# Attention and a GEGLU feed-forward block on one core: splitting each batch into an attention phase and a feed-forward phase, with tiled matmuls and hand-ordered queues

## The chip, the cores and the metric

The kernel runs on one core of a Trainium2 chip. The metric is the device time of one execution in microseconds; a profile's span (first to last instruction) is up to 3 us shorter than the timed run.

The engines are called PE (TensorE, the matrix multiplier), DVE (VectorE), ACT (ScalarE), Pool (GpSimd) and SP (SyncE). "The changed kernel" is the kernel after the change.

## The reference

```python
# attention: B, H, S, Nb, D = 8, 8, 576, 16, 64; 16 "beacon" keys that every query sees, then causal
k_all = concatenate([beacon_k, k], axis=2);  v_all = concatenate([beacon_v, v], axis=2)
scores = where(causal, -1e9, q @ k_all.T / 8)
a = softmax(scores);  x = a @ v_all                       # -> (4608 tokens, 512)
# feed-forward: d_model 512, d_ff 1536
out = (gelu(x @ w_gate) * (x @ w_val)) @ w_out            # float32
```

## The kernel before

Per batch and pair of heads it transposes q and k on PE, computes the scores with the keys on the partitions, adds the causal mask with a matmul of the identity and a mask tile, takes exp on ACT, and multiplies exp (the stationary operand) with v and a column of ones. The result has queries on partitions, so DVE normalises it and PE transposes it back. Feed-forward work for finished tokens is woven in: one "unit" (a gate and value step, or a quarter of an output chunk) after each key tile.

```python
# scores: contraction over all 128 partitions; the other head's 64 rows of q are zero
for hi in range(2):
    nc.tensor.matmul(scs[hi][0:kr, 0:width], kT_sb[0:P, jj*P : jj*P+kr],
                     qT_sb[hi][0:P, s_lo : s_lo+width], start=True, stop=not diag)
if diag:                                   # the mask, as a matmul
    for hi in range(2):
        nc.tensor.matmul(scs[hi][0:kr, 0:Nd], ident[0:kr, 0:kr], mb[0:kr, 0:Nd], start=False, stop=True)
...
# values: exp is stationary, v and a column of ones move (65 columns)
nc.tensor.matmul(x_ps[0:N, hi, :], expT[0:kr, hi, off : off+N], v_sb[0:kr, jj, 2*m+hi, :], ...)
...
nc.vector.reciprocal(...);  nc.vector.tensor_scalar(...)            # for each head
nc.tensor.transpose(xT_ps, xn_sb[0:N, :], ident[0:N, 0:N])          # back to features on partitions
nc.vector.tensor_copy(xT_sb[:, m, n0 : n0+N], xT_ps)
...
# one unit of feed-forward: g_ps and v_ps have one PSUM buffer each while attention runs
nc.scalar.activation(th_sb, g_ps, ACT.Tanh, scale=GELU_TANH_SCALE)
nc.vector.scalar_tensor_tensor(out=p_sb, in0=th_sb, scalar=1.0, in1=g_ps, op0=ALU.add, op1=ALU.mult)
nc.vector.scalar_tensor_tensor(out=hT_sb[:, fi, :], in0=p_sb, scalar=0.5, in1=v_ps, op0=ALU.mult, op1=ALU.mult)
...
for jj in range(N_KT):                     # the weaving
    attn_qk_tile(jj, qT_sb, kT_sb, expT)
    try_emit_ffn(tokens_written, 1)
    if pending:
        attn_av_chunk(*pending.pop(0))
```

The softmax here doesn't subtract the row's maximum and nothing guards it: scores larger than these inputs give would overflow.

Of the kernel before, what the change touches and what calls it, by code (L numbers as in the profile page):

```python
# [8 lines left out]
P = 128  # L9
# [5 lines left out]
N_KT = 5  # L15
N_QT = 5
F_TILES = D_FF // P
K_CHUNKS = D_MODEL // P
N_TOK_CHUNK = 512
N_CHUNKS = N_TOK // N_TOK_CHUNK  # L20
NPAIR = H // 2

S_LO = [0, 112, 240, 368, 496]
S_N = [112, 128, 128, 128, 80]
KROWS = [128, 128, 128, 128, 80]

GELU_TANH_SCALE = 0.7978845608028654

PASSES = [(0, 0, 512), (0, 512, 64), (1, 112, 464), (2, 240, 336), (3, 368, 208), (4, 496, 80)]
EXP_OFF = [0, 576, 1040, 1376, 1584]  # L30
EXP_W = 1664
QK_SCALE = 0.125
# [4 lines left out]
ALU = mybir.AluOpType  # L37


@with_exitstack  # L40
def kernel(
# [12 lines left out]
    nc = tc.nc  # L54

    const = ctx.enter_context(tc.tile_pool(name="const", bufs=1))
    wpool = ctx.enter_context(tc.tile_pool(name="wpool", bufs=1))
    xpool = ctx.enter_context(tc.tile_pool(name="xpool", bufs=1))
    inpool = ctx.enter_context(tc.tile_pool(name="inpool", bufs=3))
    tpool = ctx.enter_context(tc.tile_pool(name="tpool", bufs=2))  # L60
    epool = ctx.enter_context(tc.tile_pool(name="epool", bufs=3))
    npool = ctx.enter_context(tc.tile_pool(name="npool", bufs=4))
    fpool = ctx.enter_context(tc.tile_pool(name="fpool", bufs=2))
    hpool = ctx.enter_context(tc.tile_pool(name="hpool", bufs=2))
    opool = ctx.enter_context(tc.tile_pool(name="opool", bufs=2))

    ident = const.tile([P, P], BF16, name="ident", tag="ident")
    make_identity(nc, ident)
    NEG = -30000.0
    mb_std = const.tile([P, P], BF16, name="mb_std", tag="mb_std")  # L70
    mb0 = const.tile([P, 112], BF16, name="mb0", tag="mb0")
    nc.gpsimd.memset(mb_std, 0.0)
    nc.gpsimd.affine_select(
        out=mb_std,
        in_=mb_std,
        pattern=[[1, P]],
        compare_op=ALU.is_ge,
        fill=NEG,
        base=0,
        channel_multiplier=-1,  # L80
    )
    nc.gpsimd.memset(mb0, 0.0)
    nc.gpsimd.affine_select(
        out=mb0,
        in_=mb0,
        pattern=[[1, 112]],
        compare_op=ALU.is_ge,
        fill=NEG,
        base=16,
        channel_multiplier=-1,  # L90
    )

    wg_sb = wpool.tile([P, K_CHUNKS, D_FF], BF16, name="wg_sb", tag="wg_sb")
    wv_sb = wpool.tile([P, K_CHUNKS, D_FF], BF16, name="wv_sb", tag="wv_sb")
    wo_sb = wpool.tile([P, F_TILES, D_MODEL], BF16, name="wo_sb", tag="wo_sb")

    def load_weights():
        nc.gpsimd.dma_start(
            out=wg_sb, in_=moe_w_gate.rearrange("(kk p) f -> p kk f", p=P)
        )  # L100
        nc.gpsimd.dma_start(
            out=wv_sb, in_=moe_w_val.rearrange("(kk p) f -> p kk f", p=P)
        )
        nc.gpsimd.dma_start(
            out=wo_sb, in_=moe_w_out.rearrange("(ii p) m -> p ii m", p=P)
        )

    xT_sb = xpool.tile([P, NPAIR, N_TOK], BF16, name="xT_sb", tag="xT_sb")

    dma_jobs = []  # L110

    def load_batch(b):
        q_sb = inpool.tile([P, N_KT, H, D], BF16, name="q_sb", tag="q_sb")
        k_sb = inpool.tile([P, N_KT, H, D], BF16, name="k_sb", tag="k_sb")
        v_sb = inpool.tile([P, N_KT, H, D + 1], BF16, name="v_sb", tag="v_sb")

        def dma(out_ap, in_ap):
            nc.gpsimd.dma_start(out=out_ap, in_=in_ap)  # L118

        hsets = [(0, 2), (2, H)] if b == 0 else [(0, H)]  # L120
        nc.gpsimd.memset(v_sb[:, :, :, 64:65], 1.0)
        for (h0, h1) in hsets:
            hs = slice(h0, h1)
            for j in range(4):
                dma(q_sb[:, j, hs, :], q[b, hs, j * P : (j + 1) * P, :].rearrange("h p d -> p h d"))
            dma(q_sb[0:64, 4, hs, :], q[b, hs, 512:576, :].rearrange("h p d -> p h d"))
            dma(k_sb[0:NB, 0, hs, :], beacon_k[b, hs, :, :].rearrange("h t d -> t h d"))
            dma(k_sb[NB:P, 0, hs, :], k[b, hs, 0:112, :].rearrange("h p d -> p h d"))
            for j in range(1, 4):
                r0 = 112 + (j - 1) * P  # L130
                dma(k_sb[:, j, hs, :], k[b, hs, r0 : r0 + P, :].rearrange("h p d -> p h d"))
            dma(k_sb[0:80, 4, hs, :], k[b, hs, 496:576, :].rearrange("h p d -> p h d"))
            dma(v_sb[0:NB, 0, hs, 0:64], beacon_v[b, hs, :, :].rearrange("h t d -> t h d"))
            dma(v_sb[NB:P, 0, hs, 0:64], v[b, hs, 0:112, :].rearrange("h p d -> p h d"))
            for j in range(1, 4):
                r0 = 112 + (j - 1) * P
                dma(v_sb[:, j, hs, 0:64], v[b, hs, r0 : r0 + P, :].rearrange("h p d -> p h d"))
            dma(v_sb[0:80, 4, hs, 0:64], v[b, hs, 496:576, :].rearrange("h p d -> p h d"))
        return q_sb, k_sb, v_sb

    ph1 = ExitStack()
    ph1.__enter__()
    psum_sc = ph1.enter_context(tc.tile_pool(name="psum_sc", bufs=2, space=bass.MemoryType.PSUM))
    psum_x = ph1.enter_context(tc.tile_pool(name="psum_x", bufs=2, space=bass.MemoryType.PSUM))
    psum_gv = ph1.enter_context(tc.tile_pool(name="psum_gv", bufs=1, space=bass.MemoryType.PSUM))
    pools = {"g": (psum_gv, "g"), "v": (psum_gv, "v"), "o": (psum_x, "x")}

    qpers = ctx.enter_context(tc.tile_pool(name="qpers", bufs=1))
    qTA0_tiles = []
    qT0B_tiles = []  # L150
    for r in range(2):
        ta = qpers.tile([P, S], BF16, name=f"qTA0_{r}", tag=f"qTA0_{r}")
        tb = qpers.tile([P, S], BF16, name=f"qT0B_{r}", tag=f"qT0B_{r}")
        nc.vector.memset(ta[64:128, :], 0.0)
        nc.vector.memset(tb[0:64, :], 0.0)
        qTA0_tiles.append(ta)
        qT0B_tiles.append(tb)
    pair_counter = [0]

    def transpose_pair(q_sb, k_sb, m):  # L160
        r = pair_counter[0] % 2
        pair_counter[0] += 1
        qT_ps = psum_sc.tile([P, 1024], BF16, name="qT_ps", tag="sc0")
        for j in range(4):
            nc.tensor.transpose(
                qT_ps[:, j * P : (j + 1) * P],
                q_sb[:, j, 2 * m : 2 * m + 2, :],
                ident[:, :],
            )
        nc.tensor.transpose(  # L170
            qT_ps[:, 512:576], q_sb[0:64, 4, 2 * m : 2 * m + 2, :], ident[0:64, 0:64]
        )
        qTA0 = qTA0_tiles[r]
        qT0B = qT0B_tiles[r]
        nc.scalar.copy(qTA0[0:64, :], qT_ps[0:64, 0:S])
        nc.scalar.copy(qT0B[64:128, :], qT_ps[64:128, 0:S])  # L176
        kT_ps = psum_sc.tile([P, 1024], BF16, name="kT_ps", tag="sc1")
        for j in range(4):
            nc.tensor.transpose(
                kT_ps[:, j * P : (j + 1) * P],  # L180
                k_sb[:, j, 2 * m : 2 * m + 2, :],
                ident[:, :],
            )
        nc.tensor.transpose(
            kT_ps[:, 512:592], k_sb[0:80, 4, 2 * m : 2 * m + 2, :], ident[0:80, 0:80]
        )
        kT_sb = tpool.tile([P, SK], BF16, name="kT_sb", tag="kT_sb")
        nc.scalar.copy(kT_sb, kT_ps[:, 0:SK])  # L188
        return (qTA0, qT0B), kT_sb

    def attn_qk_pair_start():
        return epool.tile([P, 2, EXP_W], BF16, name="expT", tag="expT")

    def attn_qk_tile(jj, qT_sb, kT_sb, expT):
        kr = KROWS[jj]
        for (pj, s_lo, width) in PASSES:
            if pj != jj:
                continue
            diag = s_lo == S_LO[jj]
            Nd = S_N[jj]  # L200
            scs = [
                psum_sc.tile([P, 512], FP32, name=f"sc{hi}", tag=f"sc{hi}")
                for hi in range(2)
            ]
            for hi in range(2):
                nc.tensor.matmul(  # L206
                    scs[hi][0:kr, 0:width],
                    kT_sb[0:P, jj * P : jj * P + kr],
                    qT_sb[hi][0:P, s_lo : s_lo + width],
                    start=True,  # L210
                    stop=not diag,
                )
            if diag:
                mb = mb0 if jj == 0 else mb_std
                for hi in range(2):
                    nc.tensor.matmul(  # L216
                        scs[hi][0:kr, 0:Nd], ident[0:kr, 0:kr], mb[0:kr, 0:Nd],
                        start=False, stop=True,
                    )
# [52 lines left out]
    def ensure_transposed(b, m):  # L272
        if b >= B:
            return
# [164 lines left out]
```

## Time and profile before

484.34 us (median of 4 runs, 483.44 to 486.26); span 481.2 us.

The page of the profile. The first line gives busy time, share of the span and instruction count of each engine (PEld: weight loads; with PE they add up to 672.5 us in a span of 481.2, so the two overlap); the rows of digits are tenths of busy time, or of the granted PE clock, in 40 equal slices; in the groups, the numbers after the first bar are busy us and mean ns of one, those after the second bar the engine's idle time just before them.

```profile
PE 433.9 (90%) x3384; PEld 238.6 (50%) x3440; DVE 267.6 (56%) x1020; ACT 265.9 (55%) x625; POOL 125.0 (26%) x174
...
PE   2488699999998999989999999999998999999994
...
PEclk9999899999999999999999999999999999999998
...
L334 PE MATMUL o_ps<-wo_sb,hT_sb 128*128 128x512 bf16 x426 | 98.0, 379 | 0.9 <-DVE xT_sb L262 0.6
...
L240 PE MATMUL x_full<-v_sb,expT 128*128 128x65 bf16 (+3 forms) x960 | 60.4, 198 | 0.0
```

PE is the engine to look at, but "90% busy" does not say how much is left to gain, and the mean lengths (379 and 198 ns) do not say what a matmul costs. Records overlap: those of 379 ns start 216 ns apart. The price is the time from one start to the next, 216 ns for 512 columns and 29 ns for most value matmuls. The timeline of PE in the steady state (start us, length us, line, operation, tiles and shapes, count):

```profile
200.06 0.36 PE L206 MATMUL sc_3179<-qTA_1_120,kT_sb 128*128 128x464 bf16 x1
200.26 0.36 PE L206 MATMUL sc_3180<-qT0B_121,kT_sb 128*128 128x464 bf16 x1
200.45 0.22 PE L216 MATMUL sc_3179<-mb_std,ident 128*128 128x128 bf16 x1
200.51 0.22 PE L216 MATMUL sc_3180<-mb_std,ident 128*128 128x128 bf16 x1
200.56 0.31 PE L206 MATMUL sc_3199<-qTA_1_120,kT_sb 128*128 128x336 bf16 x1
...
205.27 0.39 PE L165 MATMUL qT_ps<-ident,q_sb 128*128 128x128 bf16 x4
205.59 0.20 PE L170 MATMUL qT_ps<-ident,q_sb 64*128 64x64 bf16 x1
205.72 0.40 PE L179 MATMUL kT_ps<-ident,k_sb 128*128 128x128 bf16 x4
```

The two heads' scores follow one another, 0.19 us for 464 columns. The second part shows something more: the transpose of q's last 64 rows is recorded with the tile 64\*128, its neighbours with 128\*128. From the start of the matmul before it to its own start pass 151 ns where 55 are usual, and to the next one 132 ns where a matmul of 64 columns takes about 28. So in this trace changing the array's tiling costs about 100 ns each way (96 and 104 here). The 80-row transpose of k that follows (80\*128) shows no such stop: it starts 56 ns after the matmul before it, at 205.96 us, and the next one 40 ns later; it is counted as no change.

A sum over the recorded starts divides the span. "Streaming" is each matmul at its ordinary start-to-start time (216 ns for 512 columns, 89 for 208, 55 to 56 for 128 in this trace, which is 2.4 columns per ns plus 2 to 3 ns; 29 ns or so for the shortest); a change of tiling is the excess at such a place, up to 105 ns; the rest of the excess is waiting. 55 of 1296 feed-forward matmuls are missing from this trace; they are added back at 0.216 us and taken off the waits.

| before, us | |
|---|---|
| feed-forward matmuls, 1296 x 0.2155 | 279 |
| scores and masks | 61 |
| value matmuls | 28 |
| transposes, in and out | 24 |
| 64 changes of tiling | 6 |
| PE waits between its first and last matmul | 71 |
| before the first matmul; after the last | 4; 6 |

About 34 us of the waits lie in the first 60 us. The busy times by stretch (columns: stretch, length, then PE, PEld, DVE, ACT and Pool busy with counts, granted clock, DMA share, GB/s):

```profile
0.00:60.00 60.00, 35.57 (x343) 22.58 (x347) 20.46 (x115) 35.02 (x87) 47.60 (x74) 0.97 1.29 120
60.00:120.00 60.00, 57.96 (x468) 32.26 (x475) 38.03 (x144) 35.32 (x82) 35.69 (x46) 1.00 1.71 128
120.00:420.00 300.00, 286.60 (x2331) 159.71 (x2371) 178.95 (x714) 178.49 (x427) 41.72 (x54) 1.00 0.34 40
```

PE has only 343 matmuls in the first 60 us; the first exp starts at 18.4 us and the first gate matmul at 51.8.

### The profile page before, as it was taken

The page shows a single profiled execution, that of the slowest core. Times are in us where ns is not written, and L with a number is a line of the kernel's source. Part 1 is how long each engine was busy: PE and PEld are TensorE (multiplying, and loading weights), DVE is VectorE, ACT ScalarE, POOL GpSimd, SP SyncE. Part 2 cuts the span into 40 slices and gives each one's busy share as a digit, 9 for nine tenths or more (in the row PEclk, how much of TensorE's full clock was granted, in tenths as well). Part 3 has the DMA queues.
Part 4 walks back from the last instruction along what each step waited for, and adds up shares of the span by engine and source line. Part 5 has one row for each costly group of instructions (what it writes and reads, how often), then busy time and mean ns, then how long its engine had stood idle before and what let it go on. Part 6 is the DMA issues. An engine that isn't in the chain of part 4 may idle for free.

```text
span 481.2 us, 8884 instructions
## 1 busy us (share of the span) xinstructions
PE 433.9 (90%) x3384; PEld 238.6 (50%) x3440; DVE 267.6 (56%) x1020; ACT 265.9 (55%) x625; POOL 125.0 (26%) x174
## 2 busy tenths in 40 slices
PE   2488699999998999989999999999998999999994
PEld 0255455555555555555555455555555554544441
DVE  0056387347843786268625783488437762782850
ACT  2388546665556755584657556655566554332321
POOL 9998129933430415040330300000000000000000
PEclk9999899999999999999999999999999999999998
DMA  4999999998592809054392800200020000200202
GB/s 28 85 119 163 206 173 126 131 157 52 36 67 80 59 2 101 0 111 29 24 78 89 52 1 0 89 1 1 1 89 1 1 0 1 90 0 1 87 1 87
DMA packets 122491, 29.16 MB, mean 61 GB/s; under 512 B 115280, under 2 KB 116816, under 8 KB 122448
## 3 DMA queue, kind: packets, MB, share of 16 engines
q0 software_dynamic: 117696, 19.15, 54.3%
q1 hardware_dynamic: 4752, 9.44, 5.2%
q8 instruction: 27, 0.44, 0.4%
q14 instruction: 16, 0.13, 0.1%
HBM read 38.27 MB, written 9.44 MB: 99 GB/s over the span
## 4 chain that ended last, share of the span: by engine, by line
PE 66%; ACT 13%; POOL 8%; DVE 6%; DMA 4%; issue 2%; ACTq 0%; POOLq 0%
PE o_ps L334 19%; PE g_ps L297 17%; PE v_ps L306 15%; ACT expT L222 4%; DVE p_sb L316 4%; DMA wv_sb<-in_moe_w_val_dram 4%; PE x_full L240 4%; ACT th_sb L314 4%; POOL v_sb L118 3%; POOL k_sb L118 3%; POOL q_sb L118 2%; PE xTf L261 1%; ACT qT0B_121 L176 1%; ACT kT_sb L188 1%; DVE hT_sb L319 1%
## 5 line engine op out<-in xcount | busy, mean ns | idle before, releaser
L297 PE MATMUL g_ps<-xT_sb,wg_sb 128*128 128x512 bf16 x394 | 109.2, 379 | 7.7 <-DMA wg_sb<-in_moe_w_gate_dram 2.3
L306 PE MATMUL v_ps<-xT_sb,wv_sb 128*128 128x512 bf16 x421 | 111.0, 379 | 1.3 <-DMA wv_sb<-in_moe_w_val_dram 0.9
L314 ACT ACTIVATE th_sb<-g_ps 128x512 bf16<-128x512 f32 x108 | 64.4, 598 | 78.4 <-PE g_ps L297 53.8
L316 DVE SCALAR_TENSOR_TENSOR p_sb<-th_sb,g_ps 128x512 bf16<-128x512 bf16 x108 | 74.1, 687 | 51.7 <-ACT th_sb L314 51.5
L334 PE MATMUL o_ps<-wo_sb,hT_sb 128*128 128x512 bf16 x426 | 98.0, 379 | 0.9 <-DVE xT_sb L262 0.6
L249 DVE RECIPROCAL rec_sb<-x_full 128x1 f32<-128x1 f32 (+2 forms) x320 | 36.5, 155 | 99.0 <-PE x_full L240 84.7
L251 DVE TENSOR_SCALAR xn_sb<-x_full,rec_sb 128x64 bf16<-128x64 f32 (+2 forms) x320 | 76.1, 278 | 0.0
L319 DVE SCALAR_TENSOR_TENSOR hT_sb<-p_sb,v_ps 128x512 bf16<-128x512 bf16 x108 | 73.2, 679 | 4.3 <-PE v_ps L306 2.5
L306 PEld LDWEIGHTS <-wv_sb 128*128 128x128 bf16 x432 | 41.6, 98 | 47.9 <-DMA wv_sb<-in_moe_w_val_dram 1.4
L297 PEld LDWEIGHTS <-wg_sb 128*128 128x128 bf16 x432 | 41.2, 97 | 47.6 <-issue 13.7
L334 PEld LDWEIGHTS <-hT_sb 128*128 128x128 bf16 x432 | 40.6, 98 | 46.0 <-issue 1.6
L240 PE MATMUL x_full<-v_sb,expT 128*128 128x65 bf16 (+3 forms) x960 | 60.4, 198 | 0.0
L240 PEld LDWEIGHTS <-expT 128*128 128x128 bf16 (+3 forms) x960 | 51.0, 108 | 17.7 <-issue 0.6
L341 ACT COPY o_sb<-o_ps 128x512 f32<-128x512 f32 x36 | 21.1, 585 | 68.4 <-PE o_ps L334 68.4
L262 DVE COPY xT_sb<-xTf 128x128 bf16<-128x128 bf16 (+2 forms) x160 | 34.4, 215 | 41.9 <-PE xTf L261 41.9
L118 POOL DMA_DIRECT2D q_sb<-in_q_dram x45 | 37.4, 893 | 47.5 <-PE qT_ps L170 47.5
L118 POOL DMA_DIRECT2D k_sb<-in_k_dram x45 | 37.4, 900 | 16.3 <-DMA wo_sb<-in_moe_w_out_dram 8.3
L216 PEld LDWEIGHTS <-ident 128*128 128x128 bf16 (+1 forms) x320 | 29.6, 103 | 17.7 <-issue 7.7
L261 PE MATMUL xTf<-ident,xn_sb 128*128 128x128 bf16 (+2 forms) x160 | 34.8, 217 | 2.6 <-DVE xn_sb L251 2.2
L118 POOL DMA_DIRECT2D v_sb<-in_v_dram x45 | 37.0, 869 | 0.0
L206 PEld LDWEIGHTS <-kT_sb 128*128 128x128 bf16 (+1 forms) x384 | 33.1, 104 | 6.3 <-issue 3.5
L261 PEld LDWEIGHTS <-xn_sb 128*128 128x128 bf16 (+2 forms) x160 | 15.6, 97 | 27.6 <-DVE xn_sb L251 17.0
(1121 smaller groups left out, 488.2 us busy)
## 6 DMA issues: line engine op xcount, KB each, us to landing
out_dram<-o_sb SPq DMA_DIRECT2D x9, 1024.0 KB, 4.4
q_sb<-in_q_dram POOLq DMA_DIRECT2D x28, 128.0 KB, 5.8
k_sb<-in_k_dram POOLq DMA_DIRECT2D x21, 128.0 KB, 4.4
v_sb<-in_v_dram POOLq DMA_DIRECT2D x21, 128.0 KB, 4.8
wg_sb<-in_moe_w_gate_dram POOLq DMA_DIRECT2D x1, 1536.0 KB, 11.5
wv_sb<-in_moe_w_val_dram POOLq DMA_DIRECT2D x1, 1536.0 KB, 18.1
wo_sb<-in_moe_w_out_dram POOLq DMA_DIRECT2D x1, 1536.0 KB, 26.1
k_sb<-in_k_dram POOLq DMA_DIRECT2D x7, 112.0 KB, 4.6
```

The costliest lines, as they stand in the source:

```text
L118: nc.gpsimd.dma_start(out=out_ap, in_=in_ap)
L240: nc.tensor.matmul(x_ps[0:N, hi, :], expT[0:kr, hi, off : off + N], v_sb[0:kr, jj, 2 * m + hi, :], start=(idx == 0), stop=(idx == ntiles - 1),
L249: nc.vector.reciprocal(rec_sb[0:N, hi : hi + 1], x_ps[0:N, hi, 64:65])
L251: nc.vector.tensor_scalar(out=xn_sb[0:N, 64 * hi : 64 * hi + 64], in0=x_ps[0:N, hi, 0:64], scalar1=rec_sb[0:N, hi : hi + 1], scalar2=None, ...
L261: nc.tensor.transpose(xT_ps, xn_sb[0:N, :], ident[0:N, 0:N])
L262: nc.vector.tensor_copy(xT_sb[:, m, n0 : n0 + N], xT_ps)
L297: nc.tensor.matmul(g_ps, wg_sb[:, kk, fi * P : (fi + 1) * P], xT_sb[:, kk, n0 : n0 + N_TOK_CHUNK], start=(kk == 0), stop=(kk == K_CHUNKS - 1),
L306: nc.tensor.matmul(v_ps, wv_sb[:, kk, fi * P : (fi + 1) * P], xT_sb[:, kk, n0 : n0 + N_TOK_CHUNK], start=(kk == 0), stop=(kk == K_CHUNKS - 1),
L314: nc.scalar.activation(th_sb, g_ps, ACT.Tanh, scale=GELU_TANH_SCALE)
L316: nc.vector.scalar_tensor_tensor(out=p_sb, in0=th_sb, scalar=1.0, in1=g_ps, op0=ALU.add, op1=ALU.mult)
L319: nc.vector.scalar_tensor_tensor(out=hT_sb[:, fi, :], in0=p_sb, scalar=0.5, in1=v_ps, op0=ALU.mult, op1=ALU.mult,)
L334: nc.tensor.matmul(o_ps, hT_sb[:, fi, ti * P : (ti + 1) * P], wo_sb[:, fi, :], start=(fi == 0), stop=(fi == F_TILES - 1),)
```

## The change

The intent: fewer streamed columns in attention, fewer and larger instructions on DVE and ACT, no masks and no back-transposes on PE, and an order of every queue written by hand. Each batch becomes an attention phase, filled with the output matmuls of the batch before, and a pure gate-and-value phase.

```diff
-# scores over 128 partitions, q padded with zeros, mask by matmul, exp per head
+# scores: each head on its own 64 rows of the array; one exp for both heads; mask afterwards on Pool
+for hi in range(2):
+    r = slice(64 * hi, 64 * hi + 64)
+    mm(s_ps[:, hi, col : col + w], qkT[r, 1, t * P : (t + 1) * P],
+       qkT[r, 0, NB + s_lo : NB + s_lo + w], True, True)
+act(expT[:, :, o : o + w], s_ps[:, :, 0:w], ACT.Exp, scale=QK_SCALE)
+keep(nc.gpsimd.affine_select(out=d, in_=d, ..., fill=0.0, ...))
...
-# values: exp stationary, [v, 1] moving; reciprocal, scale, transpose back, copy
+# values transposed: v (or ones, for the sums) stationary, exp moving; each head in its own 64 columns
+for hi in range(2):
+    mm(x_ps[64 * hi : 64 * hi + 64, base + q0 : base + q1],
+       v_sb[0:kr, t, 2 * m + hi, :] if base == X0 else ones[0:kr, :],
+       expT[0:kr, hi, e0 : e0 + q1 - q0], first and not (base == Z0 and q0 == 0), last, ...)
+act(ln_sb, x_ps[:, Z0 : Z0 + S], ACT.Ln);  act(rec_sb, ln_sb, ACT.Exp, scale=-1.0)
+keep(nc.vector.tensor_tensor(out=xT_sb[:, m, ...], in0=x_ps[:, X0 : X0 + S], in1=rec_sb, op=ALU.mult))
...
-# feed-forward: Tanh, two vector instructions, one PSUM buffer for g and one for v
+act(ge_sb, gv_ps[:, 0, :], ACT.Gelu)                       # gv_ps: both in one of two buffers
+keep(nc.vector.tensor_tensor(out=h_of[ci][:, fi, :], in0=gv_ps[:, 1, :], in1=ge_sb, op=ALU.mult))
...
+# q and k of batches 0 and 1: four sequence rows in one 1 KB read; DVE undoes the permutation
+if b < NPERM: dma(dst[...], src[b, :, 0:512, :].rearrange("h (p r) d -> p h (r d)", r=4))
...
+for m in range(1, NPAIR):                                  # the order of an attention phase
+    scores(b, m, 0); scores(b, m, 1)
+    av(m - 1, 0, 2); o(4)                                  # o(n): n output matmuls of batch b - 1
+    scores(b, m, 2); av(m - 1, 4, 1, 3)
+    if m < NPAIR - 1: transpose_pair(b, m + 1)
+    o(2); normalize(b, m - 1); scores(b, m, 3); o(2)
```

## The prediction

> **What bounds it now.** The tensor engine (PE). The engine table has PE busy 90%, vector engine 56%, scalar engine 55%. Start-to-start times in the timeline: a 512-column matmul 216 ns, a value matmul 29 ns (38 ns with 80 weight columns). Feed-forward: 1296 × 0.216 = 280 us, unchanged. Attention, per head pair: scores 3328 columns 1.4 us, 10 mask matmuls 0.5, 30 value matmuls 0.95, 10 input transposes 0.5, 5 output transposes 0.3: about 3.7 us, 32 pairs = 120 us. Before and after each 64-row transpose PE loses about 100 ns (151 ns against 55 start to start; 132 against 28); 64 such changes of array tiling cost 6 us. Together 406 of 481 us. The other 75 us are waits: some 40 in the first 60 us (first exp at 18.4 us, first gate matmul at 51.8, 10 feed-forward matmuls by 60 us), the rest spread over the middle, where gate and value products have one PSUM buffer each and tanh and two vector instructions (0.60 + 0.69 + 0.68 us) stand in the loop.
>
> **What changes on PE.** Scores of two heads go to two 64-row tiles and should run together: 1664 columns, 0.72 us. Masks and output transposes go (-0.8 us). Value matmuls stream 1664 columns of exp plus 1664 for sums against ones, two heads in two 64-column tiles: 18 slots, short ones [...] at about 65-70 ns: 1.7 us instead of 0.95. So a pair needs about 2.9 us, 93 us in all. But the program now has 409 changes of tiling instead of 64; at 0.1 us they cost 41 us. [...] PE work: 280 + 93 + 41 = 414 us, slightly more than now.
>
> **What changes elsewhere.** Vector engine: 1020 instructions become about 350, off the path. Gelu (0.6 us) plus one vector multiply (0.69) fit under a 1.73 us gate-and-value step with two buffers, so feed-forward phases run at PE's rate, 20.8 us. In attention phases the scalar engine needs 4.7 us a pair (exps of 1024, 960, 928, 416 elements at 0.17 + 0.00083 per element, then Ln and Exp of 576), PE about 6 with output matmuls between; exchanges of two PSUM buffers leave some waits (about 20 us in the whole), and the single output accumulator a few. Table loads, 1.3 us twice per batch, mostly hide. 1 KB rows and fewer issues bring the first exp to about 12.5 us.
>
> **Sum.** First attention phase ends near 38 us; 8 feed-forward phases at 20.8; 7 attention phases at about 30; last chunk and outputs about 46-49: near 461 us span, 463 us timed. Range 440 to 484. Faster by over 2%: 0.74; within 2%: 0.19; slower: 0.07.
>
> **Signs.** Phases: feed-forward 20-22 us, attention 28-32. First exp 11-14 us. Two heads' score matmuls start under 30 ns apart, and so do long value matmuls; a pair's value matmuls take 1.5-2.0 us. At each change of tiling about 0.1 us beyond streaming. PE gaps at score matmuls waiting for exp.
>
> **What would make it wrong.** Value tiles not overlapping: +35 us (about 500). Scores not overlapping: +14. Short value slots at 110 ns: +15. Changes of tiling at 60 ns: -10; free: -25. The second batch's load landing behind the weights at 45 us instead of 36: +9. Pool's 34 load issues at 0.88 us in the first feed-forward phase delaying the masks of the next batch.

That two tiles run side by side was an assumption, since no trace of the kernel before has two tiles at work together. The 65 to 70 ns for a short value slot were the author's estimate; two value matmuls of the kernel before, at 29 to 38 ns, take 58 to 76.

## The result, and the profile after

465.61 us (median of 4 runs, 465.3 to 466.41); span 463.9 us. Ratios here and below are the mean time of one kernel's fast runs over that of the other's of the same rounds, so not quite the ratio of the medians quoted: 0.961, 95% interval 0.9586 to 0.9635. The change is 3.9% faster.

The page of the changed kernel:

```profile
PE 420.9 (91%) x3248; PEld 201.6 (43%) x3248; DVE 152.7 (33%) x259; ACT 230.9 (50%) x316; POOL 164.1 (35%) x297
...
PE   0577997999999999999999999999999999999985
...
PEclk9987999999999999999999999999999999999999
...
L140 PE MATMUL o_ps<-wo_sb,hT_sb 128*128 128x512 bf16 x432 | 112.8, 381 | 6.9 <-DVE o_sb L302 6.9
...
L140 PE MATMUL x_ps<-expT,ones 128*64 128x144 bf16 (+5 forms) x576 | 49.1, 254 | 0.0
```

DVE's instructions fell from 1020 to 259 and its busy time by 115 us, yet PE is as busy as before. The clock row dips in the first slices; what lies behind that is shown with the phases below. The timeline of PE in an attention phase:

```profile
132.21 0.60 PE L140 MATMUL o_ps<-wo_sb,hT_sb 128*128 128x512 bf16 x2
132.75 0.60 PE L140 MATMUL s_ps<-qkT_101 64*128 64x512 bf16 x8
133.28 0.44 PE L140 MATMUL x_ps<-expT,v_sb_100 128*64 128x496 bf16 x4
133.55 0.41 PE L140 MATMUL x_ps<-expT,ones 128*64 128x432 bf16 x4
133.79 0.31 PE L140 MATMUL x_ps<-expT,v_sb_100 128*64 128x256 bf16 x4
133.94 0.31 PE L140 MATMUL x_ps<-expT,ones 128*64 128x192 bf16 x4
134.18 1.04 PE L140 MATMUL o_ps<-wo_sb,hT_sb 128*128 128x512 bf16 x4
```

Three tilings follow one another: 64\*128 for scores, 128\*64 for values, 128\*128 for outputs. Eight score matmuls, two of 512 columns and two of 336 among them, take 0.53 us: the two heads' matmuls start 3 to 4 ns apart. The same division of the span as above (no feed-forward matmul is missing here):

| us, rounded | before | after |
|---|---|---|
| feed-forward matmuls | 279 | 279 |
| scores (before: and masks) | 61 | 23 |
| value matmuls (after: and sums) | 28 | 47 |
| transposes | 24 | 18 |
| changes of tiling | 64: 6 | 409: 40 |
| PE waits | 71 | 41 |
| before the first; after the last | 4; 6 | 13; 4 |

The streamed work fell by 26 us, the changes of tiling took back 34, and PE's waits fell by 30; the later first matmul costs 8, the shorter end gives 2. With these rounded numbers that is 16 us, of 17 between the spans. The gain is thus a gain in waiting, and the better use of the array was about paid away at its changes.

The phases. Stretches of the changed kernel: the first attention phase, the second, a later one, and the feed-forward phase behind it (columns as above):

```profile
15.90:45.20 29.30, 22.06 (x269) 13.07 (x270) 7.88 (x18) 16.94 (x22) 20.30 (x37) 0.83 1.35 170
...
67.00:98.70 31.70, 27.24 (x310) 13.57 (x310) 10.07 (x21) 19.55 (x26) 20.70 (x38) 1.00 0.97 83
...
119.60:148.00 28.40, 26.88 (x286) 13.59 (x286) 8.08 (x15) 19.52 (x26) 10.98 (x25) 1.00 0.18 35
148.00:168.90 20.90, 20.90 (x97) 9.25 (x95) 8.97 (x13) 8.44 (x13) 10.14 (x14) 1.00 1.26 92
```

Feed-forward phases run at PE's rate: PE is busy for 20.90 of the 20.90 us. Attention phases take 28.4 us, with three exceptions: the first, at a mean granted clock of 0.83, the second, 31.7 us long, and the last, which has no next batch to transpose and takes 27.2.

The 0.83 is too high. The record of the granted clock begins at 25.27 us, and what comes before is counted as full rate. The same eight score matmuls at the start and later:

```profile
15.93 1.01 PE L140 MATMUL s_ps<-qkT_101 64*128 64x512 bf16 x8 [1.59 <-DVE qkT_101 L179]
...
126.97 0.60 PE L140 MATMUL s_ps<-qkT_103 64*128 64x512 bf16 x8
```

Likewise from one 496-column value matmul to the 80-column one behind it pass 412 ns at 22.70 us and 234 at 133.28; in the recorded windows of half the clock it is 413 (29.13 us) and 412 (35.70). So PE ran up to 25.27 us as it did in those windows, and with them for about 19 of the first phase's 29.3 us. The kernel before also starts this way: its clock record begins at 24.74 us, and at 24.0 us its 128-column matmuls start 106 to 107 ns apart, where 55 to 56 are usual.

### The profile page after: what moved, and what is told of

It is laid out like the page before. It is cut to its first block, busy times and chain, and to the rows that moved or that the text cites. A ratio compares the mean times of both kernels' runs of the same rounds, so it can differ in the third digit from the quotient of the medians.

```text
span 463.9 us, 7740 instructions
## 1 busy us (share of the span) xinstructions
PE 420.9 (91%) x3248; PEld 201.6 (43%) x3248; DVE 152.7 (33%) x259; ACT 230.9 (50%) x316; POOL 164.1 (35%) x297
## 4 chain that ended last, share of the span: by engine, by line
PE 85%; DVE 5%; ACT 4%; POOL 2%; DMA 2%; issue 1%; DVEq 0%; POOLq 0%
PE gv_ps L140 40%; PE o_ps L140 20%; PE x_ps L140 11%; PE t_ps L152 7%; PE s_ps L140 6%; DVE xT_sb L250 2%; DMA k_sb_93<-in_k_dram 2%; DVE o_sb L302 2%; ACT expT L143 2%; ACT rec_sb L143 1%; ACT ln_sb L143 1%; POOL v_sb_94 L107 1%; DVE qkT_101 L171 1%; DVE qkT_103 L171 1%; POOL q_sb_92 L107 0%
## 5 line engine op out<-in xcount | busy, mean ns | idle before, releaser
L143 ACT ACTIVATE expT<-s_ps 128x1024 bf16<-128x1024 f32 (+3 forms) x128 | 106.4, 861 | 62.0 <-PE s_ps L140 61.9
L207 POOL TENSOR_SCALAR_AFFINE_SELECT expT<-expT 128x256 bf16<-128x256 bf16 (+2 forms) x160 | 59.6, 393 | 215.9 <-ACT expT L143 215.9
L143 ACT ACTIVATE ge_sb<-gv_ps 128x512 bf16<-128x512 f32 x108 | 64.5, 597 | 123.8 <-PE gv_ps L140 123.8
L281 DVE TENSOR_TENSOR hT_sb<-gv_ps,ge_sb 128x512 bf16<-128x512 f32 x108 | 74.7, 692 | 117.5 <-ACT ge_sb L143 117.5
L140 PE MATMUL gv_ps<-xT_sb,wg_sb 128*128 128x512 bf16 x432 | 112.4, 380 | 0.6 <-DVE xT_sb L250 0.6
L140 PE MATMUL gv_ps<-xT_sb,wv_sb 128*128 128x512 bf16 x432 | 112.2, 379 | 0.0
L140 PE MATMUL x_ps<-expT,ones 128*64 128x144 bf16 (+5 forms) x576 | 49.1, 254 | 0.0
L302 DVE COPY o_sb<-o_ps 128x512 f32<-128x512 f32 x36 | 24.7, 686 | 47.0 <-PE o_ps L140 47.0
L140 PE MATMUL s_ps<-qkT_101 64*128 64x512 bf16 (+2 forms) x192 | 22.0, 297 | 4.0 <-DVE qkT_101 L179 3.3
L140 PE MATMUL x_ps<-expT,v_sb_94 128*64 128x80 bf16 (+5 forms) x216 | 20.1, 276 | 4.2 <-DVE xT_sb L250 4.1
L140 PE MATMUL s_ps<-qkT_103 64*128 64x512 bf16 (+2 forms) x192 | 20.5, 293 | 3.4 <-DVE qkT_103 L179 3.4
L140 PE MATMUL x_ps<-expT,v_sb_97 128*64 128x80 bf16 (+5 forms) x216 | 17.6, 248 | 5.0 <-DVE xT_sb L250 3.1
L152 PE MATMUL t_ps<-ident,q_sb_92 128*64 128x128 bf16 (+2 forms) x76 | 6.9, 236 | 13.0 <-POOL ident masks.py:199 12.7
```

The lines of the kernel that those rows point to most:

```text
L140: keep(nc.tensor.matmul(out_ap, lhsT, rhs, start=start, stop=stop, **kw))
L143: keep(nc.scalar.activation(out_ap, in_ap, func, **kw))
L152: keep(nc.tensor.transpose(out_ap, in_ap, ident[r0 : r0 + n, r0 : r0 + n]))
L207: nc.gpsimd.affine_select(out=d, in_=d, pattern=[[0, 2], [1, DIAG[t]]], compare_op=ALU.is_ge, fill=0.0, base=NB if t == 0 else 0, channel_ ...
L281: nc.vector.tensor_tensor(out=h_of[ci][:, fi, :], in0=gv_ps[:, 1, :], in1=ge_sb, op=ALU.mult)
L302: keep(nc.vector.tensor_copy(o_sb[:, ti, :], o_ps))
```

## The experiments

Every number of a difference below is the difference of two ratios to the kernel before, times 484.3 us, against the changed kernel's 0.961; ratios have intervals of 0.002 to 0.005 either way, 1 to 2.5 us.

Theory A: the time is PE's own path, so that each item of the table costs what PE spends on it, changes of tiling included, except where a named wait sits. Rival B: the attention phases are paced by ACT (exps) and by the hand-overs of PSUM buffers, and PE's items vanish in its waits.

### Fewer changes of tiling: whole_array_transposes

```diff
-            tr(t_ps[:, w, 512:576], src[0:64, 4, 2 * m : 2 * m + 2, :])
-        tr(t_ps[:, 1, 576:592], k_ring[b % NRING][64:80, 4, 2 * m : 2 * m + 2, :], 64)
+            tr(t_ps[:, w, 512:592], src[0:80, 4, 2 * m : 2 * m + 2, :])     # q's rows 64:80 are zeroed once
```

> The last rows of q (64) and of k with the beacons (64 + 16) are transposed as one 80-row matmul each[...], so the program has 291 changes of tiling instead of 409. Theory A (each change stops the tensor engine for about 97 ns and lies on the path): 118 x 0.097 = 11.4 us less, about 454 us. Theory B (the attention phases are paced by the exps on the scalar engine, and the tensor engine's stops fall into its waits): under 3 us, 463 to 466 us.

455.92 us, ratio 0.9412: 9.6 us less, for 118 changes fewer. That is 81 ns for each (give or take 20, from the intervals), of the 97 that stand in the records. (That an 80-row transpose is no change of tiling is what the starts show: in the kernel before as told above, and here five transposes with an 80-row one among them take 0.26 us, 171.21 to 171.47, where five with a 64-row one take 0.46 in the changed kernel, 145.30 to 145.76.) A later attention phase of this kernel, to be held against the one from 119.60 us above:

```profile
118.46:145.10 26.64, 24.43 (x277) 12.70 (x281) 8.26 (x15) 19.29 (x26) 10.59 (x24) 1.00 0.17 36
```

Attention phases fell from 28.4 to 26.6 us, 1.7 us for the 18 changes that went from each: 95 ns for one. Theory A holds, B falls: PE's stops lie on the path.

### Are the tiles really side by side? values_one_head_then_other, heads_far_apart, values_same_columns, scores_same_rows

The first idea was to set the two heads' value matmuls apart in the program, so that neighbours sit in the same columns of the array.

```diff
-                for hi in range(2):          # inside the loop over pieces
+        for hi in range(2):                  # outside it: four pieces of head 0, then four of head 1
```

> The same value matmuls, all of head 0 and then all of head 1 within each key tile, so that neighbours sit in the same 64 columns of the array and cannot run side by side. If side-by-side running is what halves the time of the value matmuls (stream 46 us in all, neighbours 3 to 4 ns apart), the stream doubles: 35 to 45 us longer, 500 to 511 us. If the records' 3 to 4 ns are only bookkeeping and the array serialises anyway: no change.

468.18 us, ratio 0.966: 2.4 us more where 35 to 45 were expected. It was the experiment that failed, not the overlap. The recorded starts (ns) of the first eight matmuls after the scores, in the order of time; the program has all four of head 0 ahead of all four of head 1:

```
program order   496  80  432  144 (head 0)   496  80  432  144 (head 1)
start, head 0   130313  130546  130581  130765
start, head 1   130326  130560  130595  130778
```

The array started head 1's first matmul 13 ns after head 0's first, ahead of three that stand before it. (The records do not name the head; head 0 is put first. Built again, the program has its matmuls in the order written, here and in the next experiment, so the build did not reorder them; a later step of the compiler was not looked at. Ends are modelled in these records, so nothing is said of them.) How many places ahead does a matmul start?

```diff
-            for t in tt:
-                attend(b, m, t)              # both heads
+            for hi in range(2):
+                for t in tt:
+                    attend(b, m, t, hi)      # 8 or 10 matmuls of head 0, then of head 1
```

> Right results. All value and sum matmuls of head 0 in a group (8 or 10), then all of head 1, so that a head-1 matmul stands 8 to 10 matmuls (16 to 20 instructions with the weight loads) behind its neighbour. With three in between, the array still started it 13 ns later and the whole cost 2.6 us. If the array looks ahead over the whole group: 466 to 472 us. If the lookahead is shorter than that: the heads partly serialise, 475 to 510.

494.6 us, ratio 1.0194: 28 us more. In a group of eight and eight, head 1's first matmul (496 columns, at 141325 ns) started 6 ns after the fifth of head 0 (256 columns, at 141319); in a group of ten and ten, 6 ns after the seventh (143994 and 143988). In both, and in the kernel before this one, it passed exactly three earlier matmuls; all groups of these shapes in the two traces show the same place.

To take the overlap away altogether, the next experiment puts both heads on the same part of the array. This gives wrong results.

```diff
-                        x_ps[64 * hi : 64 * hi + 64, base + q0 : base + q1],
+                        x_ps[0:64, base + q0 : base + q1],        # and the normalisation on 0:64 only
```

> Wrong on purpose: both heads' value and sum matmuls write PSUM partitions 0 to 63, so that they sit in the same 64 columns of the array (the normalisation reads and writes those 64 partitions only). Reordering the heads cost 2.6 us, because the array started the other column tile's matmuls 13 ns later, ahead of three that stood before them in the program. Here there is no other tile to run ahead on: if side by side running is real, the stream of 46 us doubles and the time is 38 to 48 us longer, 503 to 513; otherwise no change.

511.19 us, ratio 1.0536: 45 us more; the value stream rises from 47 to 91 us. The timeline of PE with both heads in one column tile:

```profile
153.29 0.68 PE L143 MATMUL x_ps<-expT,v_sb 128*64 128x496 bf16 x4
153.80 0.66 PE L143 MATMUL x_ps<-expT,ones 128*64 128x432 bf16 x4
154.30 0.45 PE L143 MATMUL x_ps<-expT,v_sb 128*64 128x256 bf16 x4
154.58 0.46 PE L143 MATMUL x_ps<-expT,ones 128*64 128x192 bf16 x4
```

The first row's four matmuls (496, 496, 80 and 80 columns) now reach to the next row in 0.51 us; in the changed kernel above it is 0.27.

```diff
-                r = slice(64 * hi, 64 * hi + 64)
+                r = slice(0, 64)                                  # scores of head 0, twice
```

> Wrong on purpose: both heads' scores use head 0's 64 rows, so that the same matmuls cannot sit in two row tiles. If the two row tiles run side by side in the changed kernel, the scores' stream doubles from 22.5 to about 45 us: 18 to 24 us longer, about 484 to 490. If the exps on the scalar engine pace the attention phases, much of that vanishes in the waits: under 8 us.

488.22 us, ratio 1.0062: 22 us more, and the score stream rises from 23 to 45 us. (The check of results still called it correct: with inputs this small the attention weights are nearly uniform, so a right result does not prove right scores here.) The two row tiles are worth 22 us. About 6 of them came in the first attention phase, 35.2 instead of 29.3 us, where the granted clock was one half for 20.5 us on end. The second grew by 0.1 us only, since its wait for Pool's masks (1.76 us in the changed kernel) is gone; the six later ones grew by 2.4 to 2.5 us each.

### What the output matmuls do in the attention phase: outputs_with_gates

```diff
-            if b: out_mms(b - 1, u[0], u[0] + n); u[0] += n       # o(n) in the attention phase
+            return
...
             gate_val(b, fi, kk_late=fi == 0)
+            if b: out_mms(b - 1, 4 * fi, 4 * fi + 4)
```

> The output matmuls of the batch before leave the attention phases and go between the gate and value matmuls, four to each step, as in the last chunk. 289 changes of tiling instead of 409. Theory A (without output matmuls in between, an attention phase is bound by the scalar engine's 4.8 us a pair and the hand-overs of two PSUM buffers): attention phases 22 to 25 us instead of 28.4, feed-forward phases 31.2 instead of 20.9, so 28 to 48 us longer in all, 494 to 514. Theory B (the output matmuls only lengthen the attention phases by their own time and their changes of tiling): attention phases 16 to 18 us, total 454 to 466.

523.84 us, ratio 1.0797: 57 us more, above the expected range. An attention phase and the feed-forward phase behind it:

```profile
190.10:215.00 24.90, 18.27 (x238) 10.99 (x238) 6.57 (x13) 17.61 (x23) 11.21 (x25) 0.88 0.17 20
215.00:247.20 32.20, 31.66 (x148) 14.05 (x147) 10.31 (x16) 9.96 (x16) 9.97 (x13) 0.99 0.85 75
```

An attention phase without outputs still takes 24.9 us, and PE is idle for a quarter of it; the outputs then cost 11.3 us in the other phase. Seven feed-forward phases grew by 11.2 us each (79 us); of the attention phases with outputs, six gave back 3.5 to 4.5 us (23 us) and the second grew by 2.3: 58 us between the spans. (The expectation had taken 10.3 us a phase and hoped for 22 us at the lower end of an attention phase.) Along with PE's pauses comes a second loss: the granted clock is 0.88 in this phase, 1.00 in the changed kernel's. PE's own waits in the attention phase above (us in total, times, longest):

```profile
PE x_ps L140 <- DVE xT_sb L250: 2.4, 1, 2.4
PE s_ps L140 <- DVE qkT L179: 2.2, 3, 0.7
PE s_ps L140 <- ACT expT L143: 1.2, 1, 1.2
```

Here rival B is right in part: without a filler the attention phase is bound by hand-overs, but more by those through DVE (the normalisation of a pair, behind Ln and Exp on ACT, and the copies of transposes) than by the exps, and ACT is busy for 17.6 of the 24.9 us. With the filler, PE is the limit again.

### The start: short_rows, identity_first, identity_first_loads_spread

```diff
-NPERM = 2
+NPERM = 0            # no 1 KB rows
```

> The 1 KB rows of the first two batches are taken back: all q and k in 256 B rows. q and k of a batch then are about 9200 packets instead of about 3300, and Pool issues 11 loads instead of 5 before the first scores. The landing rate of short rows was about 1000 packets per us, so the first scores should come 5 to 7 us later (22 us instead of 16), and the total be 3 to 7 us longer if the first phase is a chain of latencies; under 2 us if later loads bound the first phase anyway.

471.95 us, ratio 0.9728: 5.7 us more. The first scores start at 18.2 us instead of 15.9, the first attention phase takes 32.4 us instead of 29.3, and the second 34.4 instead of 31.7. (The phases are those of the profiled run, the slowest of four, and add up to 8 us. The landing rate in the expectation: 18543 packets under 512 B in the kernel before between 20 and 40 us, 927 per us.) The 1 KB rows earn their extra DVE copies, though only a part of it at the first scores, which came earlier than expected.

```diff
+    make_identity(nc, ident)
     load_qk(0)
     load_v(0)
-    make_identity(nc, ident)
```

> The identity is made before the loads are issued. In the trace the first transpose waited for it until 12.7 us, while q had landed by about 7.8 us and k by about 11. Theory A (the first attention phase is a chain of latencies from the first transpose on): the first transposes start near 8 to 9 us and the whole is 2 to 4 us shorter, about 462. Theory B (the first phase ends when the second batch's k lands, at about 39 us, or when the weights land): under 1 us.

465.7 us, ratio 0.9616: no change, although the first transposes start at 7.8 us instead of 12.7. The first attention phase ends 2.3 us earlier (42.9 us) and the second lasts 34.2 us instead of 31.7. Pool's and PE's timelines in that second phase, with the identity first:

```profile
66.16 4.24 POOL L107 DMA_DIRECT2D k_sb<-in_k_dram  x5
70.30 0.62 POOL L107 DMA_DIRECT2D k_sb<-in_beacon_k_dram  x1
70.83 0.61 POOL L107 DMA_DIRECT2D v_sb<-in_beacon_v_dram  x1
71.35 4.29 POOL L107 DMA_DIRECT2D v_sb<-in_v_dram  x5
75.53 2.79 POOL L207 TENSOR_SCALAR_AFFINE_SELECT expT<-expT 128x224 bf16<-128x224 bf16 x8
...
76.09 0.44 PE L140 MATMUL x_ps<-expT,v_sb 128*64 128x496 bf16 x4 [2.76 <-POOL expT L207]
```

Pool worked through its queue in program order: it issued the loads of two batches, 0.85 us for a load of 128 partitions, and only then made the masks; PE stood for 2.76 us in front of the first value matmul. In the changed kernel that wait was 1.76 us. So 1.0 of the 2.5 us is this wait; the rest falls together with a window of half the clock, 77.2 to 80.6 us, which the changed kernel does not have there. What the start gained was lost in and behind the next queue.

```diff
-                if b == 0: load_qk(2); load_v(2)
-                if b + 3 < B: load_qk(b + 3); load_v(b + 3)
+                if b + 2 < B: load_qk(b + 2); load_v(b + 2)
```

> Identity first, as before, and in each feed-forward phase the loads of one batch only (batch b + 2), where the changed kernel issues two batches' loads in the first one. The trace of identity_first has the first attention phase end 2.3 us earlier, and the second last 34.2 us instead of 31.7: Pool issued 34 loads one after the other until 75.6 us and made the second batch's masks only after that, in both kernels. Theory A (Pool's queue of loads ate the gain): the second attention phase falls to about 29 to 30 us, 4 to 5 us less in all, about 461. Theory B (the second phase is long because its transposes of permuted rows take 18 matmuls and three copies): it stays at 31 us or more, 463 to 466.

462.33 us, ratio 0.9532: 3.8 us less than the changed kernel. The second attention phase takes 29.8 us. Of the 3.3 us that it had over the later phases, 1.9 were Pool's queue. About 1.4 are left; they fit the permuted rows, with 19 matmuls and more copies in each set of transposes, but no run takes that apart.

### Waits that are left: next_transposes_first, all_repairs, all_but_output_order

```diff
-        av(m, 0, 2)
         if b + 1 < B:
             transpose_pair(b + 1, 0)
+        av(m, 0, 2)
         av(m, 4, 1, 3)
```

> At the end of each attention phase the transposes of the next batch's first pair go ahead of the last pair's first value matmuls, which in the changed kernel waited 1.0 to 1.2 us in each phase for the normalisation of the pair before (one PSUM accumulator). 12 changes of tiling go too. If that wait lies on the path: 7 x (1.1 + 0.15) = 8 to 9 us less, about 457. If the time moves into the next wait (the first gate matmuls waiting for the last pair's normalisation): under 2 us.

461.22 us, ratio 0.9507: 5.0 us less, more than half of what was expected. Attention phases take 27.2 us instead of 28.4, but the second one 33.5 instead of 31.7: PE waits 3.2 us for Pool's masks there, and a window of half the clock follows (77.1 to 80.5 us). That again took what the first phase had gained. In the last phase there are no transposes to move.

All repairs together, with two small ones more:

```diff
         scores(b, 0, 2)
-        o(4)
         transpose_pair(b, 1)
         scores(b, 0, 3)
-        o(4)
+        o(8)
...
+                if ci == N_CHUNKS - 1 and ti:       # the last chunk: four accumulators, three of them in x_ps
+                    o_of[ci][1] = x_of["last"][:, (ti - 1) * D_MODEL : ti * D_MODEL]
```

> Whole-array transposes (-9.7 us measured), identity first and loads spread (-3.3 measured), the next batch's transposes ahead of the last values (-8), in the first pair of a batch the eight output matmuls behind the last scores in one group instead of twice four (the wait of 0.65 us for the single output accumulator in each of 7 phases: -4.5), and the last chunk's outputs in four accumulators (3 x 0.7: -2). If all add: 438 us. If what one saves appears as another's wait: 442 to 450.

442.5 us (442.47 to 443.0), right results, ratio 0.9124 to the kernel before: 8.8% faster than it, and 5% faster than the changed kernel. An attention and a feed-forward phase:

```profile
158.20:184.00 25.80, 24.25 (x276) 12.85 (x281) 8.17 (x15) 19.26 (x26) 9.87 (x23) 1.00 0.12 34
184.00:205.00 21.00, 20.95 (x98) 9.29 (x97) 8.97 (x13) 8.47 (x13) 11.20 (x15) 1.00 1.35 97
```

The parts did not add up to 438. To see whether the grouping of the outputs had given anything, it alone was taken back:

> All repairs but one: the output matmuls of a batch's first pair stand again as twice four. all_repairs came to 442.5 us, about 4.5 above the sum of the parts. If grouping the eight had saved its 0.65 us in each of 7 phases, this kernel takes about 447 us and the shortfall lies elsewhere. If that wait only came back as waits for the exps (a 0.21 us wait stood before the last scores and another at the transposes), this kernel takes 441.5 to 443.5 us.

444.67 us, ratio 0.9166: neither of the two expected values. The spans differ by 2.5 us, and the phases show where. From the third on, attention phases take 25.8 to 25.9 us in both kernels: the grouping gives 0.1 us at most in each. In all_but_output_order the single accumulator's wait stands at 0.48 us in the first pair of a batch; in all_repairs there is a wait of 0.21 us for an exp instead, and the four steps up to the second pair's first scores take 6.94 and 6.88 us. In the second attention phase the grouping does give 0.9 us. There DVE has the longer copies of permuted rows to make (1.5 us for a pair in the changed kernel, 73.42 to 74.91, where 0.8 is usual, 125.90 to 126.73), and the second pair's first scores (all_but_output_order, then all_repairs) wait for them behind four output matmuls but not behind eight:

```profile
72.11 0.60 PE L142 MATMUL s_ps<-qkT 64*128 64x512 bf16 x8 [0.42 <-DVE qkT L180]
...
69.90 0.60 PE L142 MATMUL s_ps<-qkT 64*128 64x512 bf16 x8
```

They start 7.87 and 6.95 us into the phase; from there to its end both take 20.5 us. The other 1.3 us are there before that phase begins. The first attention phase (28.4 us against 27.3) has no output matmuls in either kernel; the half clock was granted at other times (6.8 us on end, into the feed-forward phase, against two windows of 3.4 us). So about half of this pair's difference comes from the start, for reasons not settled, and the grouping earned about 1 us of the 4.5 expected: in most phases it turned one wait into another. The last chunk's four accumulators gave 0.9 us of the 2 expected (from the last feed-forward chunk to the end 69.6 us instead of 70.5).

## Why the prediction was right, point by point

- **The total**: 463 us predicted, 465.61 measured; range and direction held. It is right partly because misses on the way cancel, as the following shows.
- **PE's work hardly falls**: predicted 406 to 414 us; measured (streaming plus changes of tiling in the table) 399 to 406. The count of 409 changes and their price of 0.1 us, read from 64-row transposes in the kernel before, gave 41 us; the records show 40, and the experiment with 118 fewer gave back 9.6. This was the step that kept the prediction from following the column counts, which alone promise 26 us more. The records show a stop at a change, mostly of 96 to 104 ns (about 80 behind the 16-row transposes), though not what the array does in it. That two tiles run side by side, which was an assumption in the prediction, is shown by the 22 and 45 us that it costs to deny row and column tiles (the prediction had priced these at 14 and 35).
- **Scores**: 23 us predicted (0.72 a pair), 23 measured.
- **Values**: mis-sized. Predicted 1.7 us a pair (55 us), measured 1.48 (47). The short slots were priced at 65 to 70 ns, the author's estimate; 80-column slots take 35 ns. The weight loads of the two column tiles overlap each other too (most start 3 to 4 ns apart, and one lasts about 110).
- **The first attention phase**: wrong. First exp at 12.5 us predicted, 16.6 measured; its end at 38, measured 45.2. Of the 7 us, 4 are the late first exp. The prediction missed that the identity stood behind eleven loads on Pool, but that is only 2.0 of the 4: in identity_first the first exp still comes at 14.5 us, because k lands at 11.4 and its transposes wait for it. The rest is the phase itself, where PE has no filler, waits, and runs at half the clock for about 19 of 29.3 us: up to 25.27 us, and in three recorded windows of 3.4 us.
- **Attention phases**: about 30 us predicted, 28.4 measured in five of seven (31.7 and 27.2 in the other two; 201 us together where 210 were predicted). That gave back what the first phase had lost, and most of it is the value slots, 5.9 us in a phase where 6.8 were predicted. Their waits came out about as assumed, 18 us by the division above against 20. Had the filler not been there, 24.9 us plus 11.3 elsewhere would have been the price.
- **Feed-forward phases**: 20.8 us predicted, 20.9 measured: Gelu (0.60 us) and one DVE multiply (0.69) do hide under 1.73 us of matmuls. Each load of the Gelu set takes 1.28 us; it starts 17 to 18 ns after the activation before it ends, and the first Gelu 171 to 172 ns after it, following a wait for PE; the loads of the Exp set start as soon, and the first exp 11 to 12 ns after them.
- **Pool's loads ahead of the masks** were named as a risk, and it occurred: 1.76 us of PE in the second attention phase, and more as soon as the first phase got faster.

## What to carry to other kernels

Before splitting matmuls into array tiles, count the changes of tiling that the program order makes and multiply by the 0.1 us or so that one took in these traces; here they cost more than the tiles saved, and mere reordering and padding (an 80-row transpose in place of 64 and 16 rows) took a fourth of that back. Pool's queue here issued loads (0.85 us for one of 128 partitions) as well as making masks, one behind the other: a gain at the start (2.3 us in identity_first, lost again in the next phase, 2.5 us longer) is only a gain if that queue is free to follow. And a repair is worth what the stage's last wait gives: of repairs priced at 27.5 us together, 23 arrived.
